# One saturating add in place of an add and a clamp in a seven-product MLP stage, and another instruction order, in a Sinkhorn attention, Fourier mixing and MLP kernel

## The chip, the cores and the metric

The kernel runs on one core of one Trainium2 chip. The metric is the device time of one execution in microseconds; the median of three runs is given. A core has five engines with a queue each: TensorE (PE), VectorE (DVE), ScalarE (ACT), GpSimd (POOL) and SyncE (SP). The engines run beside each other and wait for each other by semaphores. Within a queue, instructions go in their order.

## The reference

Four batches of 768 positions; 8 heads of 64, so 512 columns.

```python
P = sort_net                                  # 8 x 8 per batch and head
for _ in range(5):                            # Sinkhorn normalisation
    P = P - max(P, -1); P = exp(P)
    P = P / (sum(P, -1) + 1e-9); P = P / (sum(P, -2) + 1e-9)
k_sorted = P @ blocks(k); v_sorted = P @ blocks(v)   # 8 blocks of 96 positions
attn = softmax(q_block @ k_sorted_block.T / 8)       # each block with its own
x = attn @ v_sorted
u = x + real(fft(fft(x, axis=seq), axis=columns))
un = (u - mean(u)) / sqrt(var(u) + 1e-6)
out = u + maximum(un @ w_ch1, 0) @ w_ch2             # 512 -> 2048 -> 512
```

## The kernel before

**Stages.** For each batch: loads of q, k and v; sorting by small products with a block-diagonal matrix; scores, exponential (ACT, L1245) and "em1" (exponential minus one, L1258 on DVE or L1260 on ACT) into a buffer `eb`; the product with v and division (L1292); the Fourier transforms as products with tables (`tab`, `cs`, `dtab`, `lt`); the normalised rows `un`, transposed to `ut`; the two MLP products. The work of the next batch's attention is laid between the MLP products of the batch before.

**Buffers.** There are four `eb` buffers in one tile. Parts of each must be zero; POOL writes these zeros once at the start (L697), and every em1 into a buffer waits for them. The exponentials go through three buffers `ex`. The MLP's hidden values lie in `hr`.

**MLP.** Batches 0 and 1 take the plain first product (`ff1`, L1558). Batches 2 and 3 (`SEVEN = (2, 3)`) take `ff1_seven`: columns of the weights and halves of the input are combined beforehand, so that seven products (L1694, 128x384 each, two matmuls a product) do the work of eight. It runs in 8 pairs a batch. In a pair, three of the four results are the sum of a PSUM bank and a snapshot of another bank that ACT has copied out (`snap`, L1714, buffers `vsf`); DVE adds them into `hr` (L1702) and then clamps `hr` at zero in place (L1708). The fourth is clamped by ACT (L1732). That makes 48 adds and 48 clamps over both batches. The second product of these batches is `ff2_chunk` (L1794, with sums at L1770 and L1811).

**Order.** The code describes operations to a planner (`Plan.add`) with a cost for each engine that may do them. A table `ORDER` lists, for each engine, the numbers of the operations in the order in which its queue gets them; the planner follows it, and it also settles which of DVE and ACT does an operation that either may do. Buffers are assigned as operations come up. While PE has nothing to do at the start, the planner inserts products that nobody reads (L1973). Loads by POOL (L612) use eight semaphores in turn.

Of the kernel before, what the change touches and what calls it, by code (L numbers as in the profile page):

```python
# [8 lines left out]

# [3 lines left out]
ALU = mybir.AluOpType  # L13
# [53 lines left out]
    ),  # L67
    "ACT": (
# [24 lines left out]
    ),  # L93
    "DVE": (
# [72 lines left out]
       [(7, ER[1]), (6, ER[1] + 128)],  # L167
       [(6, ER[1] + 256), (5, ER[1] + 384)],
       [(5, ER[1] + 512), (4, ER[1] + 640)]]
GT = 384  # L170


def _consts():
# [314 lines left out]
def kernel(  # L488
# [20 lines left out]
    P = Plan()  # L509
# [1496 lines left out]
```

## Time and profile before

| | |
|---|---|
| three runs, median (lowest to highest) | 257.49 us (257.4 to 257.72) |
| span of the profiled execution | 254.8 us; its whole time is not listed apart from the three runs, the difference to their median is 2.7 us |
| PE busy | 245.2 us, 96% |
| DVE busy | 234.2 us, 92% |
| ACT busy | 165.3 us, 65% |
| POOL busy | 57.5 us, 23% |
| DMA | 26.54 MB, mean 104 GB/s |
| granted clock of PE | full, except in the last slice |

Busy time is what an engine's instructions took; waiting for a semaphore, register and branch instructions don't count. A row of the time line gives start, length, engine, line, operation, what is written from what is read, and in brackets the idle time ahead of it with the instruction that ended it. In a row of groups the number behind the busy time is the mean length of one instruction in ns.

### The profile page before, as it was taken

Reading aid. Unit: us, or ns where it says so; the run is one execution under the profiler, and the core shown is the slowest. Engines: PE = TensorE matmul, PEld = TensorE weight load, DVE = VectorE, ACT = ScalarE, POOL = GpSimd, SP = SyncE. Lnnn points to the kernel's source line nnn. Section 1 sums busy time; section 2 is a strip of 40 time slices with the busy share of each in tenths; the row PEclk is TensorE's granted clock in tenths of the full one; section 3 lists DMA queues with packets and bytes.
Section 4 is the critical chain, followed back from the end, with each engine's and each line's share of the span. In section 5 each row is a group of like instructions: output and inputs, shape, how many; then the busy total and the mean of one; then the engine's idle time right before and its main releaser. Section 6 shows DMA issues by size and latency. Waiting matters only on the chain.

```text
span 254.8 us, 7461 instructions
## 1 busy us (share of the span) xinstructions
PE 245.2 (96%) x2996; PEld 167.0 (66%) x2996; DVE 234.2 (92%) x597; ACT 165.3 (65%) x376; POOL 57.5 (23%) x88
## 2 busy tenths in 40 slices
PE   4999999999999999999999999999999999999992
PEld 1347875566566676644667757888657887567882
DVE  4799998999999989978999998999999999999993
ACT  2599998999968879956797377622687323773000
POOL 8974532234400770003100000210100000050013
PEclk9999999999999999999999999999999999999998
DMA  6999999999942699524132002530202400220025
GB/s 134 202 215 300 210 217 214 208 211 187 150 49 75 86 193 120 64 43 136 44 38 44 1 8 46 98 125 35 82 3 41 84 3 0 85 88 37 3 82 207
DMA packets 42809, 26.54 MB, mean 104 GB/s; under 512 B 30234, under 2 KB 39208, under 8 KB 42772
## 3 DMA queue, kind: packets, MB, share of 16 engines
q0 software_dynamic: 23664, 18.35, 42.9%
q1 hardware_dynamic: 19110, 7.71, 15.0%
q8 instruction: 23, 0.38, 0.6%
q14 instruction: 12, 0.10, 0.1%
HBM read 29.07 MB, written 6.29 MB: 139 GB/s over the span
## 4 chain that ended last, share of the span: by engine, by line
PE 71%; issue 9%; DVE 9%; ACT 8%; POOL 2%; DMA 1%; POOLq 0%; DVEq 0%
PE bank L1558 15%; PE bank L1794 14%; PE bank L1694 12%; PE bank L1615 9%; PE bank L1275 4%; PE bank L1440 3%; PE bank L945 2%; PE bank L1236 2%; ACT vcx L855 2%; PE bank L1349 2%; POOL out_dram L1593 2%; DVE rt L1292 1%; PE bank L1444 1%; PE bank L1047 1%; PE bank L1140 1%
## 5 line engine op out<-in xcount | busy, mean ns | idle before, releaser
L1558 PE MATMUL bank<-ut,w1sb 128*128 128x384 f16 x256 | 48.2, 326 | 0.0
L1714 ACT COPY vsf<-bank 128x384 f32<-128x384 f32 x48 | 21.6, 482 | 24.0 <-PE bank L1694 23.6
L1245 ACT ACTIVATE ex<-bank 96x384 f32<-96x384 f32 x64 | 29.3, 487 | 7.6 <-PE bank L1236 6.2
L1558 PEld LDWEIGHTS <-w1sb 128*128 128x128 f16 x256 | 23.1, 98 | 14.1 <-issue 0.3
L1570 ACT ACTIVATE hr<-bank 128x384 f16<-128x384 f32 x56 | 26.3, 491 | 8.5 <-PE bank L1558 8.5
L1593 POOL DMA_INDIRECT out_dram<-u,rows x9 | 9.4, 1042 | 97.4 <-DVE u L1811 72.5
L1794 PEld LDWEIGHTS <-hr 128*128 128x128 f16 x288 | 28.2, 98 | 4.6
L1702 DVE TENSOR_TENSOR hr<-bank,vsf 128x384 f16<-128x384 f32 x48 | 25.2, 548 | 1.6 <-PE bank L1694 1.0
L1615 PE MATMUL bank<-w2sb,hr 128*128 128x512 f16 x96 | 23.6, 380 | 0.0
L1794 PEld LDWEIGHTS <-vcx 128*128 128x128 f16 x216 | 21.1, 98 | 3.2
L1694 PE MATMUL bank<-ut,w1sb 128*128 128x384 f16 x96 | 20.7, 326 | 0.0
L1794 PE MATMUL bank<-w2sb,hr 128*128 128x256 f16 x144 | 18.7, 272 | 0.0
L1275 PEld LDWEIGHTS <-eb 97*128 97x128 f16 x416 | 15.7, 98 | 3.1 <-issue 0.4
L1794 PE MATMUL bank<-kq,vcx 128*128 128x256 f16 x144 | 17.5, 272 | 0.0
L1694 PEld LDWEIGHTS <-w1sb 128*128 128x128 f16 x128 | 12.5, 98 | 7.5
L612 POOL DMA_DIRECT2D kq<-in_q_dram x18 | 15.4, 866 | 8.8 <-PE bank L1558 4.2
L1292 DVE TENSOR_TENSOR rt<-bank,rz 128x384 f16<-128x384 f32 x32 | 16.9, 547 | 0.2
L1275 PE MATMUL bank<-vsf,eb 97*128 97x65 f16 x416 | 16.9, 193 | 0.0
L855 ACT CAST ks<-bank 128x384 f16<-128x384 f32 x27 | 14.4, 555 | 3.1 <-PE bank L1140 3.0
L1260 ACT ACTIVATE eb<-ex,negone 96x384 f16<-96x384 f32 x26 | 15.9, 616 | 0.1
L855 ACT CAST vsf<-bank 96x512 f16<-96x512 f32 x22 | 14.2, 679 | 1.4 <-PE bank L945 1.4
L1258 DVE TENSOR_SCALAR eb<-ex 96x384 f16<-96x384 f32 x38 | 13.9, 371 | 0.6 <-ACT ex L1245 0.4
(195 smaller groups left out, 535.5 us busy)
## 6 DMA issues: line engine op xcount, KB each, us to landing
w1sb<-in_moe_w_ch_dram POOLq DMA_DIRECT2D x4, 512.0 KB, 18.6
w2sb<-in_moe_w_ch_dram POOLq DMA_DIRECT2D x4, 512.0 KB, 21.5
hr<-in_v_dram POOLq DMA_DIRECT2D x2, 768.0 KB, 8.8
kq<-in_v_dram POOLq DMA_DIRECT2D x2, 768.0 KB, 12.7
kq<-in_k_dram POOLq DMA_DIRECT2D x8, 192.0 KB, 6.5
kq<-in_q_dram POOLq DMA_DIRECT2D x16, 96.0 KB, 6.7
out_dram<-u SPq DMA_DIRECT2D x5, 256.0 KB
kq<-in_k_dram POOLq DMA_DIRECT2D x2, 384.0 KB, 11.7
```

The costliest lines, as they stand in the source:

```text
L855: (nc.scalar.copy if e == "ACT" else V.tensor_copy)(dst, src)
L1245: nc.scalar.activation(ex.ap[0:96], pss[h2].ap[0:96, 0:384], AF.Exp, scale=SCALE),
L1260: nc.scalar.activation(ed, src, AF.Identity, bias=negone[0:96])
L1275: nc.tensor.matmul(po.ap[:, 65 * T:65 * T + 65], eb.ap[:, e0:e0 + 128], vsf[0:97, vi:vi + 65], start=(n == 0), stop=(n == len(WIN[T]) - 1) ...
L1292: P.add({"DVE": (0.465, 0.56)}, lambda _: V.tensor_tensor(rt.ap[:, :, D * h:D * h + D], po3()[:, :, 0:D], rz.ap[:, :, None].broadcast_to([ ...
L1558: nc.tensor.matmul(ps.ap[:, 0:GT], w1sb[:, c, 128 * fc:128 * fc + 128], ut.ap[:, c, :], start=(c == 0), stop=(c == 3))
L1570: nc.scalar.activation(hr[g][:, fc, :], ps.ap[:, 0:GT], AF.Relu)
L1615: nc.tensor.matmul(ps.ap, hr[g][:, fc, 128 * tt:128 * tt + 128], w2sb[:, fc, :], start=(fc == 0), stop=(fc == 15))
L1694: nc.tensor.matmul(ps.ap[:, 0:GT], lhs[:, c, fi], rhs()[:, c, :], start=(start and c == 0), stop=(c == 1), skip_group_check=True)
L1702: return P.add({"DVE": (0.47, 0.57)}, lambda _: V.tensor_tensor(hr[g][:, fc, :], p.ap[:, 0:GT], o.ap, op=ALU.add), r=r, w=hk(g, fc, fc + 1 ...
L1714: P.add({"ACT": act(GT)}, lambda _: nc.scalar.copy(x.ap, A.ap[:, 0:GT]), r=[A], w=[x], prio=pr_v - 1, tag="pc", after=avs)
L1794: nc.tensor.matmul(ps.ap[:, o:o + 256], lhs()[:, fc], rhs[:, fc], start=(start and fc == 0), stop=(fc == 7), skip_group_check=True)
```

## The change

In `ff1_seven` the add becomes one custom VectorE instruction, which adds its inputs and limits the sum to the range 0 to the largest float; the clamp behind it is dropped. The planner's cost of the add stays. The table `ORDER` is replaced for all five engines; with it, some operations change between DVE and ACT. Line numbers fall by 2 in the first part of the file and by 7 to 10 behind the edit (the add is L1700 now).

```diff
+from concourse.dve_ops import TENSOR_ADD_SAT
...
 ORDER = {
     "PE": (
-        "77 69 78 73 79 91 139 123 125 127 92 97 129 211 141 143 0 103 218 "
+        "77 69 78 73 79 91 92 139 141 123 97 211 127 125 143 218 101 129 145 "
...
+FMAX = float(np.finfo(np.float32).max)
...
             def add(g, fc, p, o, r):
-                return P.add({"DVE": (0.47, 0.57)}, lambda _: V.tensor_tensor(
-                    hr[g][:, fc, :], p.ap[:, 0:GT], o.ap,
-                    op=ALU.add), r=r, w=hk(g, fc, fc + 1), prio=pr_v,
-                    tag="fadd")
-
-            def relu(g, fc):
-                P.add({"DVE": (0.16, 0.24)}, lambda _: V.tensor_scalar(
-                    hr[g][:, fc, :], hr[g][:, fc, :], 0.0, None, op0=ALU.max),
-                    r=hk(g, fc, fc + 1), w=hk(g, fc, fc + 1), prio=pr_v,
-                    tag="relu")
+                return P.add({"DVE": (0.47, 0.57)}, lambda _: V._custom_dve(
+                    TENSOR_ADD_SAT, out=hr[g][:, fc, :], in0=p.ap[:, 0:GT],
+                    in1=o.ap, s0=FMAX, s1=0.0), r=r,
+                    w=hk(g, fc, fc + 1), prio=pr_v, tag="fadd")
...
             add(0, i, D, x, [D, x])
-            relu(0, i)
...
             add(1, i + 8, Q, x, [Q, x])
-            relu(1, i + 8)
...
             add(1, i, Q, x2, [Q, x2])
-            relu(1, i)
```

What the two changes make of the queues is shown at three places. The first is POOL's queue at the start of the program, before. `DMASW0` to `DMASW7` are the eight semaphores of its loads; `eb_76` is the tile with the four `eb` buffers:

```order
L701 MEMSET ks_78 128x8x32
L703 MEMSET vsf 96x128
L697 MEMSET eb_76 96x1672 x4
L709 MEMSET negone 128x1
L705 MEMSET pmt 128x3x2
L612 DMA kq<-in_k_dram 128x4x384
L612 DMA kq<-in_q_dram 128x4x384
L612 DMA vcx<-k_dtab 128x1024
L612 DMA vcx<-k_lt 97x770
L612 DMA cs<-k_cs 128x2316 [waits DMASW0_49]
L612 DMA tab<-k_tab 128x1028 [waits DMASW1_49]
L612 DMA perm<-k_perm 128x136 [waits DMASW2_49]
```

And the piece of POOL's queue now that begins with the eighth load; one memset of `eb` stands ahead of it, behind the third load:

```order
L610 DMA vcx<-k_dtab 128x1024
L701 MEMSET vsf 96x128
L610 DMA vcx<-k_lt 97x770 [waits DMASW0_49]
L610 DMA hr_73<-in_q_dram 128x4x384 [waits DMASW1_49]
L610 DMA cs<-k_cs 128x2316 [waits DMASW2_49]
L610 DMA kq<-in_v_dram 128x3072 [waits DMASW3_49]
L695 MEMSET eb_76 96x1672
L610 DMA perm<-k_perm 128x136 [waits DMASW4_49]
L610 DMA w1sb<-in_moe_w_ch_dram 128x2048 [waits DMASW5_49]
L610 DMA hr_73<-in_q_dram 128x4x384 [waits DMASW6_49,PE_49]
L610 DMA hr_73<-in_k_dram 64x4x384 [waits DMASW7_49]
L695 MEMSET eb_76 96x1672 x2
```

The four memsets stood in one row ahead of the loads that wait. Now one is early, one stands behind the 12th load, and two behind the 16th; the load of `tab` has moved from the 10th to the 6th place, ahead of this piece.

The second place is DVE's queue around the first em1 instructions (L1258), before; `ex_82` to `ex_84` are the three buffers of exponentials, `vsf` takes the sorted values:

```order
L1028 TENSOR_TENSOR un_100<-un_99 128x128 [waits DVE_49]
L985 TENSOR_TENSOR bdv_1_113<-bank_63,pack 128x128
L1028 TENSOR_TENSOR un_100<-un_99 128x128
L1258 TENSOR_SCALAR eb_76<-ex_84 96x4x96 [waits Activation_49]
L1070 SCALAR_TENSOR_TENSOR rr<-ex_83,pack,bank_62 64x512 [waits Activation_49]
L1258 TENSOR_SCALAR eb_76<-ex_82 96x4x96 [waits Activation_49]
L855 CAST vsf<-bank_66 96x64x8 [waits PE_49]
L855 COPY qt_79<-bank_65 128x768 [waits PE_49,Activation_49]
L855 COPY rv<-rr 64x1 [waits DVE_49]
L1258 TENSOR_SCALAR eb_76<-ex_84 96x4x96
```

And now, where em1 is L1256:

```order
L1068 SCALAR_TENSOR_TENSOR rr<-ex_82,pack,bank_63 64x512 [waits Activation_49]
L853 COPY vcx<-hr_72 128x96x8
L1256 TENSOR_SCALAR eb_76<-ex_83 96x4x96 [waits Activation_49,Pool_49]
L853 CAST vsf<-bank_66 96x64x8 [waits PE_49]
L1256 TENSOR_SCALAR eb_76<-ex_84 96x4x96 [waits Activation_49]
L853 COPY rv<-rr 64x256 [waits DVE_49]
L853 CAST vsf<-bank_65 96x64x8 [waits PE_49]
L1256 TENSOR_SCALAR eb_76<-ex_83 96x4x96 [waits Activation_49,Pool_49]
L1256 TENSOR_SCALAR eb_76<-ex_84 96x4x96 [waits Activation_49]
L853 CAST vsf<-bank_66 96x64x8 [waits PE_49]
L1256 TENSOR_SCALAR eb_76<-ex_82 96x4x96
```

The third em1 of DVE (the fourth row from the end of the piece) waits for POOL now, with the casts of `vsf` and all further em1 behind it. Before, only DVE's first em1, ahead of the piece shown, had a wait for POOL.

The third place is DVE's queue in the seven-product stage, before: adds (L1702) and clamps (L1708) into `hr_72` and `hr_73`:

```order
L1708 TENSOR_SCALAR hr_73<-hr_73 128x384
L1702 TENSOR_TENSOR hr_73<-bank_68,vsf 128x384
L1708 TENSOR_SCALAR hr_73<-hr_73 128x384
L1702 TENSOR_TENSOR hr_72<-bank_65,vsf 128x384 [waits PE_49,Activation_49]
L1496 BN_AGGR mv_130<-st_127 128x2 [waits DVE_49]
L1702 TENSOR_TENSOR hr_72<-bank_63,vsf 128x384 [waits PE_49,Activation_49]
L1708 TENSOR_SCALAR hr_73<-hr_73 128x384
L1708 TENSOR_SCALAR hr_73<-hr_73 128x384 [waits DVE_49]
L1708 TENSOR_SCALAR hr_72<-hr_72 128x384 [waits DVE_49]
L1702 TENSOR_TENSOR hr_73<-bank_68,vsf 128x384 [waits PE_49]
```

And now, where `ISA` is the saturating add:

```order
L1700 ISA hr_73<-bank_64,vsf 128x384 [waits PE_49]
L1492 BN_STATS st_126<-u_95 128x6 [waits DVE_49]
L1700 ISA hr_73<-bank_68,vsf 128x384 [waits PE_49]
L1700 ISA hr_72<-bank_66,vsf 128x384
L1700 ISA hr_73<-bank_64,vsf 128x384 [waits PE_49]
L1465 SCALAR_TENSOR_TENSOR u_98<-rt_86,bank_62 128x510 [waits DMASW0_49,PE_49]
L1700 ISA hr_72<-bank_68,vsf 128x384 [waits PE_49]
L1474 SCALAR_TENSOR_TENSOR u_98<-rt_86,bank_62 128x2 [waits DVE_49]
L1700 ISA hr_72<-bank_66,vsf 128x384 [waits PE_49,Activation_49]
```

No clamp stands between the adds any more. Over the whole program DVE has 35 instructions fewer: the 48 clamps are gone, and about a dozen casts, em1 and others have come from ACT, one clamp of the plain first product has gone there. ACT has one more load of its function table, between the second and the third exponential of the Sinkhorn normalisation.

198 rows, old and new, of the table ORDER are left out of this document.

## The prediction

> **What bounds the kernel now.** I read the page first (shares and groups), then the table of windows, then the chain of waits in order of time, and last the time lines of VectorE (DVE) and GpSimd (POOL) in the stretches that the change touches.
>
> ```profile
> span 254.8 us, 7461 instructions
> PE 245.2 (96%) x2996; PEld 167.0 (66%) x2996; DVE 234.2 (92%) x597; ACT 165.3 (65%) x376; POOL 57.5 (23%) x88
> ```
>
> PE and DVE both look like bounds, but shares over the whole span don't say which one holds where. The windows do. The columns are PE, PEld, DVE, ACT and POOL busy, then the clock of PE:
>
> ```profile
> 24.56:49.44 24.88, 24.42 (x472) 16.59 (x469) 23.32 (x70) 23.18 (x56) 8.17 (x13) 1.00 1.14 212
> ...
> 51.00:135.00 84.00, 83.89 (x1348) 52.25 (x1348) 78.35 (x176) 68.68 (x161) 20.02 (x28) 1.00 0.84 107
> 135.00:250.00 115.00, 115.00 (x939) 86.52 (x938) 111.17 (x290) 55.37 (x128) 9.43 (x17) 1.00 0.18 50
> ```
>
> From 51 us on PE is idle for 0.11 us in 199. That it is really at work there, and not held by late operands, the chain shows in the seven-product stage (matmuls of 384 columns in one row of it):
>
> ```profile
> 216.32 10.41 PE bank L1694 x64
> ...
> 250.30 0.42 DVE L1811 TENSOR_TENSOR u<-bank,u 128x256 f32<-128x256 f32 x1 [0.34 <-PE bank L1794]
> 250.75 0.33 SPq L1583 DMA_DIRECT2D out_dram<-u  x1
> ```
>
> 10.41/64 = 0.163 us per matmul, one after the other. After PE's last product one DVE sum and one store follow. So the end is: the moment at which PE can begin its unbroken run, plus a fixed amount of matmul work, plus a tail. The run begins with the first product of the first MLP (L1558), and ahead of it stand the transposed activations that DVE copies out:
>
> ```profile
> 49.44 1.09 DVE L855 COPY ut<-bank 128x512 f16<-128x512 f16 x3 [0.28 <-PE bank L1537]
> ...
> 50.96 1.47 PE L1558 MATMUL bank<-ut,w1sb 128*128 128x384 f16 x8
> ```
>
> Before that (the first window above) DVE is busy 23.32 and ACT 23.18 of 24.88 us: the two together are the bound of the start, with 1.56 and 1.70 us of idle time.
>
> **The fused instruction.** These are the two groups that become one, and how three clamps stand in a row:
>
> ```profile
> L1702 DVE TENSOR_TENSOR hr<-bank,vsf 128x384 f16<-128x384 f32 x48 | 25.2, 548 | 1.6 <-PE bank L1694 1.0 <-ACT vsf L1714 0.3
> L1708 DVE TENSOR_SCALAR hr<-hr 128x384 f16<-128x384 f16 x48 | 10.3, 250 | 0.1
> L1453 DVE SCALAR_TENSOR_TENSOR u<-rt,bank 128x512 f32<-128x512 f16 x9 | 6.1, 680 | 0.8 <-ACT qt L855 0.5 <-PE bank L1444 0.2
> L1622 DVE TENSOR_TENSOR u<-bank,u 128x512 f32<-128x512 f32 x6 | 4.1, 687 | 1.6 <-PE bank L1615 1.6
> ...
> 189.63 0.58 DVE L1708 TENSOR_SCALAR hr<-hr 128x384 f16<-128x384 f16 x3
> ...
> 193.54 1.02 DVE L1702 TENSOR_TENSOR hr<-bank,vsf 128x384 f16<-128x384 f32 x2
> ```
>
> Three clamps take 0.58 us, so each follows the last by (0.58 - 0.25)/2 = 0.165 us: 48 of them free 48 x 0.165 = 8 us of DVE's queue. No row shows a saturating add. The nearest ones: L1453 (two arithmetic operations on two inputs) takes 680 ns for 512 elements where L1622 (one operation, same size) takes 687, so a second operation in the same pass costs nothing there. I take 548 ns, with bounds of 470 (two adds take 1.02 us, so the second follows 0.47 behind the first) and 548 + 250 = 798 ns. All 48 lie after 160 us, where the window gives PE 115.00 of 115.00: PE hides them. So 8 us off DVE are worth 0 at the end, as long as PE stays full; nor is there a wait of PE for DVE in that stretch that could go.
>
> **The new order, start.** Here the sum is made. Each em1 (L1258: exponential minus one, into one of four buffers `eb`) needs that buffer's zeros, set once by POOL (L697). Before, the four memsets stood together ahead of every load that waits:
>
> ```profile
> 4.79 6.16 POOL L697 MEMSET eb<- 96x1672 f16 x4
> ...
> 16.45 0.88 POOL L612 DMA_DIRECT2D hr<-in_k_dram  x1 [0.73 <-DMA kq<-in_q_dram]
> 18.38 0.62 POOL L612 DMA_DIRECT2D hr<-in_k_dram  x1 [1.04 <-DMA kq<-in_k_dram]
> 20.51 0.75 POOL L612 DMA_DIRECT2D hr<-in_q_dram  x1 [1.50 <-DMA kq<-in_q_dram]
> 21.60 1.23 POOL L612 DMA_DIRECT2D hr<-in_k_dram  x2 [0.34 <-DVE un L1028]
> 23.24 0.75 POOL L612 DMA_DIRECT2D hr<-in_q_dram  x1 [0.42 <-DMA cs<-k_cs]
> 26.21 1.15 POOL L612 DMA_DIRECT2D kq<-in_v_dram  x2 [2.21 <-DMA tab<-k_tab]
> ```
>
> They are done at 10.95, 1.54 us each. The rows below them show the other half of the matter: POOL's 12th, 13th and 14th load wait for the landing of its 4th, 5th and 6th, the 17th and 18th for the 9th (cs) and 10th (tab). A load waits for the one eight places ahead of it, and POOL stands still meanwhile. Now two of the memsets stand behind the 16th load, hence behind the landing of the 8th, which has become dtab; and tab has moved from 10th to 6th place. When does dtab land? Sizes and VectorE's rows:
>
> ```profile
> kq<-in_q_dram POOLq DMA_DIRECT2D x2, 384.0 KB, 10.7
> cs<-k_cs POOLq DMA_DIRECT2D x1, 579.0 KB, 8.9
> tab<-k_tab POOLq DMA_DIRECT2D x1, 514.0 KB, 11.3
> vcx<-k_dtab POOLq DMA_DIRECT2D x1, 256.0 KB, 8.4
> ...
> 24.56 0.34 DVE L1258 TENSOR_SCALAR eb<-ex 96x384 f16<-96x384 f32 x1
> ```
>
> The first five loads are as before, so the 5th is in at 18.38. Then tab: between cs's rate (23.24 - 21.60 = 1.64 us for 579 KB, so 1.46 for 514) and its own time before (26.21 - 23.24 = 2.97). Then q: 20.51 - 18.38 = 2.13. Then dtab: at most 21.60 - 20.51 = 1.09. The 16th load may go at 18.38 + 1.46 + 2.13 + 1.09 = 23.06, or with 2.97 at 24.57. Issue 0.62, two memsets 3.08: the zeros are there at 26.8 to 28.3. The first memset of the two frees an em1 of ACT, the second the third em1 of DVE. The work on DVE ahead of that one is that which stood ahead of the em1 at 24.56 before (one copy of a whole `vcx` half more, other pieces less), so DVE comes to it at about 24.5 and stands for 2.2 to 3.7 us. I take 2.6, in the lower part, since the 1.09 holds a wait for `un`. Queued behind it on DVE are all further em1, the casts of `vsf` and the divisions; ACT's next exponential needs the `ex` buffer that this em1 reads (three buffers), so ACT stops as well.
>
> [...]
>
> From there to the three `ut` copies the order gives DVE more than before: two em1, one normalisation `un` and one copy of `qt`, less one cast of `vsf`.
>
> ```profile
> L1258 DVE TENSOR_SCALAR eb<-ex 96x384 f16<-96x384 f32 x38 | 13.9, 371 | 0.6 <-ACT ex L1245 0.4
> L1522 DVE TENSOR_SCALAR un<-u,mv,ny 128x512 f16<-128x512 f32 x8 | 4.2, 530 | 0.0
> L855 DVE CAST vsf<-bank 96x512 f16<-96x512 f32 x10 | 6.8, 684 | 0.2
> 42.62 0.55 DVE L855 COPY qt<-bank 128x384 f16<-128x384 f16 x1
> ```
>
> 0.74 + 0.53 + 0.55 - 0.68 = 1.1 by durations, about 0.9 as neighbours overlap by some 0.1 us. Against it stands the idle time of DVE in that window, 1.56 us, which a late start may swallow. First product: + 2.6 + 0.9 - 1.5 = + 2.0 us. Bounds: 2.2 + 0.9 - 1.56 = + 1.5, and 3.7 + 0.9 with nothing swallowed = + 4.6.
>
> **The rest.** ACT gets one more table load (1.28 us), between the second and third exponential of the first normalisation. It fits a wait that is there:
>
> ```profile
> 0.74 1.28 ACT L711 ACT_TABLE_LOAD   x1 [0.74 <-PEq L1990]
> 6.34 0.26 ACT L766 ACTIVATE hr<-hr 32x64 f32<-32x64 f32 x1 [1.51 <-DVE hr L776]
> ```
>
> 1.51 - 1.28 leaves 0.2 us, so it costs 0; uncovered, 1.28. PE gets the same products, eight fewer of the products that only fill its idle start, and as many of its own ahead of the first L1558. Behind it PE has no idle time to give back beyond 0.11 us. The tail keeps its form: 0.
>
> Sum: 257.49 + 2.0 = 259.5 us. The profiled execution's span is 254.8; its whole time isn't listed apart from the three runs, so I carry the 2.7 us around it over unchanged, and expect a span of 256.8.
>
> **The rivals.**
> *The zeros come in time, and the new order is simply tighter* (faster). For it: the planner's order takes some DVE work out of the second group's way, and 1.56 us of DVE idle time in the start could go. It decides where the 16th load goes by 20.8 (24.5 - 3.08 - 0.62): tab, q and dtab would have to land within 2.4 us, half the time that the rows give them. Then + 0.9 - 1.56 = - 0.7: 256.8 us. Chance 0.22.
> *Stall and slack cancel*: zeros at about 25.2, a stall of 0.7, + 0.7 + 0.9 - 1.56 = 0: 257.5 us, with PE as the wall. Chance 0.10.
> *The saturating add is dear.* It is slower than before only above 548 + 165 = 713 ns, where it takes back what the clamps freed; at 798 ns it is 48 x 0.085 = 4.1 us more on a DVE that is busy for 111.17 of 115 us there, so about 0.3 us beyond its slack, with the waits of single matmuls some 1 us, on top of the forecast's + 2.0: 260.5. Chance 0.05.
> *Memsets and VectorE's copies block each other.* Two memsets of 1.54 us now stand between loads, while DVE does its four `vcx` copies. If each holds one copy up for its whole length, 3.1 us come on top of DVE's path, less 1.56 of idle time already counted: some + 1.5 beyond the forecast, 261.0. Before, no such copy met a memset, so no row decides. Chance 0.08.
> [...]
>
> **How the numbers follow.** The forecast of a stall of 1.5 to 4.6 us at the end has 0.55, and the time is its likeliest value, 259.5. The first rival reaches down to 256.8, the bound above to 257.5 + 4.6 = 262.1. The range 256.6 to 262.0 holds all rivals' values and leaves out only their far ends. A measurement of this kernel can tell about 0.2%, or 0.5 us, from no change. Faster: 0.22. The same: 0.10. Slower: 0.55 + 0.05 + 0.08 = 0.68.
>
> **What would show it.** Right: on POOL two memsets of `eb` after 23 us; a DVE em1 at about 24.5 whose row names a POOL memset, with some 2.6 us of idle time; the first L1558 at about 53; PE full from there on; saturating adds of about 548 ns; as many us between the first L1558 and the end as before (203.8 of the span). Wrong: no such wait or one below 0.7 us, a first L1558 at or before 51, or a distance from it to the end that has changed by more than 1 us; the last would mean that PE's run was not as closed as the windows say, and that the freed 8 us of DVE counted after all.

## The result, and the profile after

The changed kernel takes 261.2 us (median of 4 runs, 259.65 to 263.12) against 257.48 us (257.4 to 257.72): 1.0146 times the time before, with a 95% interval of 1.0100 to 1.0192. It is slower by 3.7 us, and its runs lie 3.5 us apart where those of the kernel before lie 0.3 us apart.

The profiled execution took 261.2 us with a span of 259.4 us. (Other runs of the kernel before have spans of 255.7 us at 257.5 us, so 1.8 us lie around a span; the span of 254.8 that the prediction used came from a run about 1 us shorter than the median.)

The table of windows, first in steps of 2 us from 22 to 34 us, then from the first MLP product on (columns as before: PE, PEld, DVE, ACT and POOL busy, the clock of PE, DMA):

```profile
22.00:24.00 2.00, 2.00 (x53) 1.55 (x45) 2.00 (x4) 1.73 (x4) 1.63 (x3) 1.00 1.21 305
24.00:26.00 2.00, 0.34 (x6) 0.14 (x3) 2.00 (x1) 0.00 (x0) 2.00 (x2) 1.00 1.13 286
26.00:28.00 2.00, 0.48 (x13) 0.39 (x13) 2.00 (x5) 1.02 (x2) 2.00 (x4) 1.00 1.01 210
28.00:30.00 2.00, 2.00 (x23) 1.39 (x20) 2.00 (x6) 2.00 (x6) 0.41 (x1) 0.50 1.05 217
30.00:32.00 2.00, 2.00 (x25) 1.93 (x23) 0.81 (x3) 1.10 (x3) 1.09 (x2) 0.64 1.16 202
32.00:34.00 2.00, 2.00 (x55) 1.70 (x53) 2.00 (x10) 1.76 (x4) 0.63 (x1) 1.00 1.30 196
...
55.00:135.00 80.00, 79.41 (x1252) 50.16 (x1245) 75.25 (x170) 59.04 (x140) 17.93 (x26) 1.00 0.81 97
135.00:255.00 120.00, 119.64 (x1020) 89.13 (x1017) 112.35 (x257) 59.34 (x137) 10.10 (x17) 1.00 0.18 52
```

From 24 to 28 us PE works 0.82 of 4 us and ACT 1.02. DVE counts as busy all the time, but with one instruction from 24 to 26. Behind the gap PE's clock is granted at 0.50 and 0.64. The time lines of POOL, DVE, ACT and PE say what happened:

```profile
22.37 0.80 POOL L610 DMA_DIRECT2D hr<-in_q_dram  x1 [1.75 <-PE bank L1234]
23.16 0.65 POOL L610 DMA_DIRECT2D hr<-in_k_dram  x1
23.78 2.96 POOL L695 MEMSET eb<- 96x1672 f16 x2
...
22.31 0.34 DVE L1256 TENSOR_SCALAR eb<-ex 96x384 f16<-96x384 f32 x1
22.58 0.68 DVE L853 CAST vsf<-bank 96x512 f16<-96x512 f32 x1
23.18 3.77 DVE L1256 TENSOR_SCALAR eb<-ex 96x384 f16<-96x384 f32 x1
26.87 0.20 DVE L853 COPY rv<-rr 64x256 f16<-64x256 f16 x1
27.00 0.68 DVE L853 CAST vsf<-bank 96x512 f16<-96x512 f32 x1
27.60 0.67 DVE L1256 TENSOR_SCALAR eb<-ex 96x384 f16<-96x384 f32 x2
...
26.98 0.49 ACT L1243 ACTIVATE ex<-bank 96x384 f32<-96x384 f32 x1 [3.24 <-DVE eb L1256]
...
27.52 0.36 PE L1168 MATMUL bank<-bdk,kq 128*64 128x128 f16 x6 [3.18 <-ACT ex L1243]
29.07 2.25 PE L1045 MATMUL bank<-tab,un 128*64 128x129 f32 x13
...
31.80 0.43 DVE L853 CAST hi<-bank 128x257 f16<-128x257 f32 x1 [1.19 <-PE bank L1045]
...
54.99 2.29 PE L1556 MATMUL bank<-ut,w1sb 128*128 128x384 f16 x13
```

The two memsets behind the 16th load run from 23.78 to 26.74. An em1 that is 0.34 us long elsewhere starts at 23.18 and ends at 26.95, 0.2 us behind them. It is DVE's second em1, the one that has no wait for POOL in its queue. ACT waits 3.24 us for the `ex` buffer that this em1 reads, PE 3.18 us for ACT. Then the 13 products L1045 take 2.25 us at the lower clock, and DVE waits another 1.19 us for them. The first MLP product comes at 54.99 instead of 50.96.

The fused instruction in the groups:

```profile
L1700 DVE CUSTOM_DVE_ANT_0 hr<-bank,vsf 128x384 f16<-128x384 f32 x48 | 24.9, 550 | 3.4 <-PE bank L1692 2.9
```

### The profile page after: what moved, and what is told of

Its sections match the earlier page's. It is cut to its first block, busy times and chain, and to the rows that moved or that the text cites. A ratio compares the mean times of both kernels' runs of the same rounds, so it can differ in the third digit from the quotient of the medians.

```text
span 259.4 us, 7377 instructions
## 1 busy us (share of the span) xinstructions
PE 245.0 (94%) x2988; PEld 168.4 (65%) x2988; DVE 235.4 (91%) x562; ACT 160.8 (62%) x364; POOL 57.5 (22%) x88
## 3 DMA queue, kind: packets, MB, share of 16 engines
HBM read 29.07 MB, written 6.29 MB: 136 GB/s over the span
## 4 chain that ended last, share of the span: by engine, by line
PE 63%; DVE 18%; issue 8%; ACT 4%; DMA 3%; POOL 2%; POOLq 0%; DVEq 0%; ACTq 0%
PE bank L1784 14%; PE bank L1692 13%; PE bank L1556 12%; PE bank L1613 5%; PE bank L1273 3%; DVE vcx L907 3%; DMA hr<-in_v_dram 3%; DVE eb L1256 3%; PE bank L1438 2%; PE bank L1347 2%; DVE rt L1290 2%; PE bank L1234 2%; POOL out_dram L1591 2%; PE bank L1045 2%; PE bank L943 2%
## 5 line engine op out<-in xcount | busy, mean ns | idle before, releaser
L1556 PE MATMUL bank<-ut,w1sb 128*128 128x384 f16 x256 | 47.4, 326 | 0.1
L1568 ACT ACTIVATE hr<-bank 128x384 f16<-128x384 f32 x57 | 26.7, 491 | 10.5 <-PE bank L1556 10.3
L1700 DVE CUSTOM_DVE_ANT_0 hr<-bank,vsf 128x384 f16<-128x384 f32 x48 | 24.9, 550 | 3.4 <-PE bank L1692 2.9
L1692 PE MATMUL bank<-ut,w1sb 128*128 128x384 f16 x96 | 20.8, 326 | 0.0
L1256 DVE TENSOR_SCALAR eb<-ex 96x384 f16<-96x384 f32 x40 | 17.3, 449 | 0.9 <-ACT ex L1243 0.7
L1273 PE MATMUL bank<-vsf,eb 97*128 97x65 f16 x416 | 17.5, 194 | 0.0
L610 POOL DMA_DIRECT2D kq<-in_q_dram x18 | 15.1, 856 | 7.9 <-DMA w2sb<-in_moe_w_ch_dram 4.9
L1591 POOL DMA_INDIRECT out_dram<-eb,rows x3 | 3.3, 1090 | 55.2 <-DVE eb L1801 45.3
L1258 ACT ACTIVATE eb<-ex,negone 96x384 f16<-96x384 f32 x24 | 14.7, 617 | 0.0
L1692 PE MATMUL bank<-qt,kq 128*128 128x384 f16 x64 | 14.6, 326 | 0.0
```

The source lines that it names most:

```text
L1256: V.tensor_scalar(ed, src, -1.0, None, op0=ALU.add)
L1273: nc.tensor.matmul(po.ap[:, 65 * T:65 * T + 65], eb.ap[:, e0:e0 + 128], vsf[0:97, vi:vi + 65], start=(n == 0), stop=(n == len(WIN[T]) - 1) ...
L1556: nc.tensor.matmul(ps.ap[:, 0:GT], w1sb[:, c, 128 * fc:128 * fc + 128], ut.ap[:, c, :], start=(c == 0), stop=(c == 3))
L1568: nc.scalar.activation(hr[g][:, fc, :], ps.ap[:, 0:GT], AF.Relu)
L1591: st_ = [nc.gpsimd.indirect_dma_start(out.rearrange("b s m -> (b s) m"), bass.IndirectOffsetOnAxis(ap=rows[:, i:i + 1], axis=0), u.ap, None)]
L1692: nc.tensor.matmul(ps.ap[:, 0:GT], lhs[:, c, fi], rhs()[:, c, :], start=(start and c == 0), stop=(c == 1), skip_group_check=True)
```

## The experiments

**Zeros early.** When the instructions are written out in their order, the first memset of `eb` brings the three others along:

```diff
+            if o.tag == "ebz":
+                zeros.append(o)
+                if len(zeros) == 1:
+                    for n in range(4):
+                        nc.gpsimd.memset(eb4[0:96, n, :], 0.0)
+                continue
             o.fn(o.eng)
```

> The changed kernel, with all four memsets of eb issued where its first one stands (after the third load on POOL); nothing else is moved. [...] If the new order itself is the loss, the time stays above 259.5.

Measured: 256.47 us, 0.9964 times the time before (0.9949 to 0.9978). The long em1 and the low clock are gone (POOL's and DVE's time lines, then the windows):

```profile
22.12 0.82 POOL L610 DMA_DIRECT2D hr<-in_q_dram  x1 [1.30 <-PE bank L949]
22.93 1.31 POOL L610 DMA_DIRECT2D hr<-in_k_dram  x2
...
22.55 0.55 DVE L1256 TENSOR_SCALAR eb<-ex 96x384 f16<-96x384 f32 x1
23.61 0.34 DVE L1256 TENSOR_SCALAR eb<-ex 96x384 f16<-96x384 f32 x1
...
24.00:26.00 2.00, 1.99 (x37) 1.35 (x36) 2.00 (x6) 2.00 (x6) 0.80 (x2) 1.00 1.11 282
```

So the place of the memsets is the whole loss, and without it the new order is 1.0 us faster than the old one. This kernel beats both. The first MLP product comes at 50.5. POOL's loads are still issued beside the first two em1: the first takes 0.55 us there, the second 0.34 as elsewhere.

**Memsets that nobody waits for.** The run before, with two memsets of the same size at the late place, into a part of `w2sb` that is not in use yet:

```diff
+                if len(zeros) > 2:
+                    nc.gpsimd.memset(idle[:, EW * (len(zeros) - 3):
+                                          EW * (len(zeros) - 2)], 0.0)
```

> As the run before, and two memsets of the same size at the old late place, behind the 16th load, into a part of w2sb that nothing reads before it is loaded 12 us later. No em1 waits for them. If the semaphore (third em1 waiting for the zeros) is the mechanism, the time is that of the run before, within 0.5 us. If a memset on POOL keeps VectorE off memory while it runs, an em1 or copy of 3 us stands again on DVE near 23 us and the time is 259.5 to 263 as in the changed kernel.

Measured: 261.64 us, 1.0179 (1.0155 to 1.0203). POOL and DVE:

```profile
23.41 0.65 POOL L610 DMA_DIRECT2D hr<-in_k_dram  x1
24.03 2.96 POOL L1975 MEMSET w2sb<- 96x1672 f16 x2
...
23.42 3.78 DVE L1256 TENSOR_SCALAR eb<-ex 96x384 f16<-96x384 f32 x1
```

No semaphore ties that em1 to these memsets, and the stall is the same: 3.78 us, where the changed kernel has 3.77. It is VectorE held off beside POOL's work, here a load's issue of 0.65 us and 2.96 us of memsets, not a wait for the zeros.

**The same memsets in pieces**, 8 of 209 elements for each:

```diff
-                    nc.gpsimd.memset(idle[:, EW * (len(zeros) - 3):
-                                          EW * (len(zeros) - 2)], 0.0)
+                    for n in range(8):
+                        nc.gpsimd.memset(idle[:, EW * (len(zeros) - 3) + 209 * n:
+                                              EW * (len(zeros) - 3) + 209 * n + 209], 0.0)
```

> The zeros early, and the two idle memsets each cut into 8 of 209 elements. If a memset holds VectorE off for the length of one instruction and lets it in between two, no em1 is longer than about 0.6 us and the time is 256.3 to 257.5. If POOL keeps VectorE out as long as it has work queued, the em1 is as long as all 16 pieces together, 3 us or more, and the time is 261 or more.

Measured: 262.34 us (259.18 to 262.9), 1.0161 (1.0094 to 1.0229). One of the four runs took 259.18 us at a mean clock of 1.00, the other three 262.2 to 262.9 at 0.982 or 0.983; the trace is that of 262.9.

```profile
23.63 3.53 POOL L1976 MEMSET w2sb<- 96x209 f16 x16
...
23.79 3.59 DVE L1256 TENSOR_SCALAR eb<-ex 96x384 f16<-96x384 f32 x1
```

The em1 ends 0.2 us after the last of 16 pieces: it found no way in between two of them. Cutting the memsets in pieces didn't help in this trace, where POOL always had the next one at hand.

**One memset in place of two** (`if len(zeros) > 3`, and one memset):

> The zeros early, and one idle memset in place of two. The held em1 takes about 2.2 us. If each us of stall costs its own length and the clock is granted in full after so short a gap of PE, the time is 256.5 + 1.5 = 258.0; if the clock drops here too, 259 or more.

Measured: 259.65 us, 1.0094 (1.0058 to 1.0131). That is 3.2 us above the kernel with early zeros, for one memset of 1.53 us:

```profile
22.14 0.81 POOL L610 DMA_DIRECT2D hr<-in_q_dram  x1 [1.30 <-PE bank L949]
22.94 0.65 POOL L610 DMA_DIRECT2D hr<-in_k_dram  x1
23.56 1.53 POOL L1975 MEMSET w2sb<- 96x1672 f16 x1
...
22.56 2.74 DVE L1256 TENSOR_SCALAR eb<-ex 96x384 f16<-96x384 f32 x1
...
25.88 0.36 PE L1168 MATMUL bank<-bdk,kq 128*64 128x128 f16 x6 [2.03 <-ACT ex L1243]
27.93 1.26 PE L1045 MATMUL bank<-tab,un 128*64 128x129 f32 x13
```

Here the first em1 is caught, at 22.56, while POOL issues a load; it ends at 25.30, after the second load's issue and the memset. So the hold can begin with the issue of a load ahead of the memset. What an issue does by itself is less clear. With zeros early the same em1, beside the same two issues but with a third one behind them in place of the memset, took 0.55 us. With the memsets in pieces it took 0.69 and got through before the memsets began. The second em1 with zeros early took 0.34 beside an issue. Why it was held through here and not there stays open. My two cases didn't hold: the em1 was 2.7, not 2.2 us, and the profiled run lost 3.1 us though the clock did not fall behind the gap (the 13 products L1045 take 1.26 us).

**The old order with late idle memsets**, behind its 17th load:

```diff
             o.fn(o.eng)
+            if o.tag == "load" and o.eng == "POOL":
+                loads += 1
+                if loads == 17:
+                    for n in range(2):
+                        nc.gpsimd.memset(idle[:, EW * n:EW * n + EW], 0.0)
```

> The kernel before in its old order, with two idle memsets of 1.5 us behind its 17th load, at 24 us. If the loss is VectorE held off by POOL's memsets and nothing special to the new order, an em1 near 24.5 us takes about 3.3 us and the time is 260 to 262. If it needs the new order, 257.5.

Measured: 259.51 us, 1.0084 (1.0062 to 1.0106), 2.6 us more, a little less than expected. An em1 at 24.88 takes 2.73 us beside memsets from 24.45 to 27.39. The loss doesn't need the new order:

```profile
24.45 2.94 POOL L1984 MEMSET w2sb<- 96x1672 f16 x2
...
23.94 0.96 DVE L855 COPY qt<-bank 128x768 f16<-128x768 f16 x1 [0.23 <-PE bank L1205]
24.82 0.14 DVE L855 COPY rv<-rr 64x1 f16<-64x1 f16 x1
24.88 2.73 DVE L1258 TENSOR_SCALAR eb<-ex 96x384 f16<-96x384 f32 x1
...
28.26 1.83 PE L1047 MATMUL bank<-tab,un 128*64 128x129 f32 x13 [1.68 <-DVE vsf L855]
...
30.00:32.00 2.00, 2.00 (x28) 1.79 (x26) 1.48 (x4) 1.73 (x6) 1.06 (x3) 0.50 1.26 223
```

The copy out of a PSUM bank at 23.94, its last 0.45 us beside the memset, takes 0.96 us and the copy of a single element a row 0.14 us, as long as in the kernel before without one; the em1 takes 2.73 us, where it is 0.34 us long in the kernel before. Behind PE's gap of 1.68 us the clock falls to 0.50 here too.

**The gap on PE filled.** The changed kernel, with 15 products that nobody reads ahead of the product that waited:

```diff
+            if o.tag == "kq":
+                groups += 1
+                if groups == 6:
+                    for _ in range(15):
+                        nc.tensor.matmul(
+                            spin.ap[:, 0:480], idh,
+                            pack[:, 0:240].bitcast(F16))
             o.fn(o.eng)
```

> The changed kernel, with 15 products that nobody reads (0.2 us each) on PE ahead of the product L1168 that waited 3.2 us. They fill PE's idle time and leave VectorE's stall as it is. If the halved clock after the gap is a second price of the stall, the clock stays 1.00 from 26 to 34 us, the 13 products L1045 take 1.3 instead of 2.3 us, and the time is 1 to 2 us below the changed kernel's, with less spread. If the clock costs nothing, the time is that of the changed kernel.

Measured: 260.41 us (259.46 to 260.55), 1.0129 (1.0107 to 1.0151). That is 0.8 us below the changed kernel's median, but not clear of noise: against the kernel before, measured beside each, the ratios are 1.0129 and 1.0146, and their intervals overlap. What did change is a mean clock of 0.995 to 1.00 where the changed kernel has 0.982 to 0.991, and a spread of 1.1 instead of 3.5 us. Its trace holds a surprise:

```profile
23.43 0.63 POOL L610 DMA_DIRECT2D hr<-in_k_dram  x1 [0.26 <-DMA vcx<-k_dtab]
24.05 2.94 POOL L695 MEMSET eb<- 96x1672 f16 x2
...
23.17 0.34 DVE L1256 TENSOR_SCALAR eb<-ex 96x384 f16<-96x384 f32 x1
23.57 0.69 DVE L853 CAST vsf<-bank 96x512 f16<-96x512 f32 x1
27.02 0.70 DVE L1256 TENSOR_SCALAR eb<-ex 96x384 f16<-96x384 f32 x2 [2.77 <-POOL eb L695]
...
28.42 1.26 PE L1045 MATMUL bank<-tab,un 128*64 128x129 f32 x13
```

In this run dtab landed 0.6 us later (15.1 us after its issue, where it was 14.5) and POOL stood still for 0.26 us. The second em1 slipped through, and the third one waited 2.77 us for the zeros, by the semaphore. Both mechanisms end with the same memset, so one takes the place of the other. The 13 products L1045 take 1.26 us again, and the first MLP product comes at 53.4. So this trace differs from that of the changed kernel in two things: the clock, and a stall of DVE of 2.77 us in place of 3.4 (3.77 less the em1's own 0.34).

**The changed kernel once more**, for a second trace:

> The changed kernel once more, unchanged, for a second trace. If VectorE is always held off by the row of POOL's work, the second em1 is again 3 us or more long. If it depends on a gap in POOL's work, the second em1 may be short and the third one wait for the zeros for 2 to 3 us, at the same time within the spread of 259.6 to 263.1.

Measured: 261.09 us (two runs), 1.0142 (1.0107 to 1.0178). The second em1 is 3.78 us long again, and the clock is low for longer, so that the first MLP product comes at 56.0, 1.0 us later than in the first trace behind the same stall:

```profile
26.00:28.00 2.00, 0.52 (x8) 0.35 (x8) 2.00 (x5) 1.06 (x2) 2.00 (x4) 0.73 1.03 214
28.00:30.00 2.00, 2.00 (x21) 1.40 (x21) 2.00 (x5) 1.81 (x6) 0.36 (x1) 0.50 1.04 215
30.00:32.00 2.00, 2.00 (x19) 1.99 (x18) 0.57 (x2) 1.35 (x3) 1.09 (x2) 0.50 1.17 202
32.00:34.00 2.00, 2.00 (x31) 1.61 (x28) 1.20 (x5) 1.09 (x2) 0.63 (x1) 0.56 1.30 196
```

**The fused instruction alone, in the old order**: `add` as in the change; the clamp's operation stays in the plan and issues nothing.

```diff
-                P.add({"DVE": (0.16, 0.24)}, lambda _: V.tensor_scalar(
-                    hr[g][:, fc, :], hr[g][:, fc, :], 0.0, None, op0=ALU.max),
+                P.add({"DVE": (0.16, 0.24)}, lambda _: None,
```

> The kernel before in its old order, with the saturating add in place of the add and with the clamps not issued. If PE is the wall after 51 us, the time is 257.5 within 0.5 us, though DVE has 48 instructions and about 8 us less. If DVE's queue counted in the seven-product stage, it is faster by 1 us or more.

Measured: 257.49 us, 0.9999 (0.9990 to 1.0009), with 104.08 us of DVE work from 135 to 250 us instead of 111.17. 7.1 us less on VectorE bought nothing there.

**The new order unfused, and the old order with clamps placed alike.** Two runs, with the clamp issued right behind its add:

```diff
-                return P.add({"DVE": (0.47, 0.57)}, lambda _: V._custom_dve(
-                    TENSOR_ADD_SAT, out=hr[g][:, fc, :], in0=p.ap[:, 0:GT],
-                    in1=o.ap, s0=FMAX, s1=0.0), r=r,
+                return P.add({"DVE": (0.47, 0.57)}, lambda _: (
+                    V.tensor_tensor(hr[g][:, fc, :], p.ap[:, 0:GT], o.ap,
+                                    op=ALU.add),
+                    V.tensor_scalar(hr[g][:, fc, :], hr[g][:, fc, :], 0.0,
+                                    None, op0=ALU.max)), r=r,
```

> The changed kernel in its new order, with add and clamp as two instructions, the clamp right behind each add. If the order is the whole loss, the time is 259.5 to 263 like the changed kernel's. If the new order relies on the 8 us freed on DVE, it is 2 us or more above the changed kernel.

> The kernel before in its old order, unfused, but with each clamp issued right behind its add, as in the run of the new order unfused. If that run lost 8 us because the new order leaves VectorE no room for 48 clamps, this one stays within 1 us of 257.5. If it lost them because a clamp right behind its add is badly placed, this one loses several us too.

Measured: 269.29 us in the new order, 1.0450 (1.0394 to 1.0505), 8.1 us above the changed kernel; 260.98 us in the old one, 1.0139 (1.0121 to 1.0157), 3.5 us above the kernel before. From 135 to 250 us (the new order, then the old one):

```profile
135.00:250.00 115.00, 109.55 (x895) 76.78 (x892) 109.85 (x276) 58.47 (x135) 4.81 (x8) 1.00 0.15 38
...
135.00:250.00 115.00, 113.79 (x910) 83.60 (x910) 111.35 (x283) 55.39 (x128) 7.05 (x12) 1.00 0.16 44
```

PE is idle for 5.45 and for 1.21 us there, where it is idle for 0.00 in the kernel before; in the old order that is only a part of the 3.5 us. A clamp right behind its add is badly placed in both orders: the 48 clamps cost VectorE 12.6 and 12.8 us of work and 1.7 and 1.6 us of idle time ahead of them, where the kernel before has 10.3 and 0.1. The bad place is the same in both, but the new order loses 8.1 us and the old one 3.5. That fits a new order that uses the room which the fusion made and leaves VectorE too little for 48 clamps. It is not shown by itself, since no run put well placed clamps into the new order. Either/or, as I had put it, was too simple.

## Why the prediction was right, and where its steps were not

**Direction and place** were right: two late memsets of `eb` behind the 16th load stop DVE, with ACT and PE behind it, and the delay reaches the end. First product + 4.03 us (54.99 for 50.96), where about 53 was expected, and from it to the end of the span 204.4 us, against 203.8 expected.

**POOL's queue** came at the time that was worked out, but by another wait. The 16th load went at 23.16 (forecast 23.06 to 24.57), the zeros were there at 26.74 (26.8 to 28.3). The forecast made it wait for dtab; dtab had landed 14.5 us after its issue at 8.01, at about 22.5. What POOL did wait for, 1.75 us, is PE's L1234 (the row at 22.37), ahead of the 15th load; the 16th followed it without a pause. The sum of landings left that wait out, so that its lower bound was met within 0.1 us is luck.

**The wait's mechanism** was not the one that the forecast priced. By the prediction's own sign ("no such wait") its semaphore failed in the changed kernel: no DVE row there names a POOL memset. What stopped DVE in both traces of the changed kernel is nearest to the rival to which I gave 0.08: VectorE held up beside POOL's memsets (an em1 of 3.77 and of 3.78 us, each beside 2.96 us of them), on an em1 and not on the `vcx` copies on which I had placed it. That rival's 3.1 us, two memsets that each hold one copy up for its whole length, no run shows; the traces show one em1 held across both memsets. Nor does a row show that VectorE holds POOL up: the two memsets take 2.96 us beside the em1, where four took 6.16 us in the kernel before. The stall cost 3.77 - 0.35 = 3.4 us, where I had 2.6 for the semaphore. The semaphore's wait is real, 2.77 us in the run with fillers, but in the two traces of the changed kernel DVE is stopped one em1 sooner. I had priced the two as adding up; they take each other's place, since both end with the second memset. That is also why the time came out in the range although the wait did not: the place of the memsets set the end of either stall. That it came within 0.2 us of that rival's 261.0 is luck, since the rival's sum held the forecast's wait as well.

How far the hold reaches, the traces show in part: the held em1 took 3.77 us beside 2.96 us of memsets, and its row starts 0.6 us ahead of them, beside the issue of a load. It isn't bound to a single instruction of POOL: with 16 short memsets in a row (3.53 us) the em1 still took 3.59 us. What in the two engines makes the one wait for the other, no run shows.

**The step that failed by its size** is the sum from the stall to the first product: "+ 2.6 + 0.9 - 1.5 = + 2.0". Its first term was 3.4. Its other two, together - 0.6, are what is left with zeros early, where nothing stalls: the first product came at 50.5 for 50.96, about - 0.4. And it held no term for PE's clock. 3.4 - 0.4 makes + 3.0, and the trace has + 4.0; the 1.0 us that is left is what the 13 products L1045 took more at the low clock (2.25 for 1.26 us). In the second trace, with the same stall and the clock low for longer, the first product came at 56.0, which by the same sum puts the clock at some 2 us there. With PE's gap filled, the clock stayed at 1.00 and the first product came at 53.4, + 2.4, which is 2.77 - 0.4. Of the 1.6 us between that run and the changed kernel, then, about 0.6 is the shorter stall and 1.0 the clock. The low clock also goes with the spread: the changed kernel's runs at 259.65, 261.2 and 263.12 us have mean clocks of 0.991, 0.988 and 0.982. Why the same gap costs the clock more in one run than in another was not tried.

The windows show the clock at 0.50 behind gaps of PE of 3.18 us in the changed kernel and of 1.68 us in the old order with late memsets, and at 1.00 behind a gap of 2.03 us in the profiled run with one idle memset. So the length of the gap alone doesn't settle whether the clock falls; what does, no run shows.

**The faster rival** had the right price, and its condition didn't hold in the changed kernel: with the zeros in time it gave 256.8, and early zeros measured 256.47. How much of the 1.0 us to the kernel before comes from the start and how much from the room on VectorE later stays open. In the two traces the first product comes 0.4 us sooner (50.5 for 50.96) and the way from it to the end is the same, 203.8 us, but the trace before is of a run faster than its median.

**The fused instruction** was right: 550 ns for a forecast of 548, and 0 at the end in the old order. That it is worth nothing is shown for the old order only. In the new order, going back to add and clamp cost 8.1 us, of which the clamps' bad place is an unknown part.

## What to carry to other kernels

Before moving anything onto POOL into a stretch where VectorE is busy, count POOL's run of work without a pause, memsets and a load issue right ahead of them together: here an em1 of 0.34 us was held for nearly all of a load's issue of 0.65 us and 2.96 us of memsets, with no semaphore to show for it, as one instruction of 3.77 us. A stall that empties PE in passing can be paid twice: here the clock fell to 0.50 behind a gap of 3.18 us, and 13 products took 2.25 us instead of 1.26. Products that nobody reads, put into that gap, kept the clock at 1.00 from 22 to 34 us, though their gain of 0.8 us was not clear of noise. And when an order is searched anew, ask what the planner has no cost for: here it was VectorE held off beside POOL's memsets, an em1 of 3.77 us, and it took more than the 1.0 us that the new order gains without it.

## What the runs showed of the hardware

- An em1 on VectorE was held across POOL's instruction boundaries: it took 3.59 us beside 16 memsets of 0.22 us. An em1 that began in a pause of 0.26 us in POOL's row took its usual 0.34 us.
- Not every VectorE instruction is held: in the changed kernel L930, which reads no PSUM bank either, took 0.69 us at 18.30 beside a memset from 17.42 to 18.93, and 0.67 us at 29.07 without one.
- The hold can begin with the issue of a load that a memset follows: in the run with one idle memset an em1 took 2.74 us, across two issues (0.81 and 0.65) and a memset (1.53). Beside issues with no memset behind them, em1 took 0.55 and 0.34 us.
- The clock of PE fell to 0.50 after gaps of 3.18 and 1.68 us, and in the profiled run with a gap of 2.03 us it did not fall (the 13 products L1045 took 1.26 us).
- The custom saturating add of two f32 inputs, one from PSUM, took 550 ns for 128x384, the plain add 548.
